# Routed attention and a SiLU layer on one core: the steps of a written-out plan in a new order

## The chip, the cores and the metric

The kernel runs on one core of a Trainium2 chip. The metric is the device time of one execution in microseconds. The core has five engines, each with its own queue of instructions worked off in order: TensorE (PE, matmuls; PEld are its weight loads), VectorE (DVE), ScalarE (ACT), GpSimd (POOL) and SyncE (SP), which here issues the transfers of the DMA engines.

## The reference

Attention in which a query sees only the keys of its own cluster, and after it two matmuls with a SiLU between them:

```
q, k, v: [4, 8, 768, 64]    centroids: [8, 16, 64]
q_assign = argmax over c of (q / |q|) . (centroid / |centroid|)      # k_assign likewise
scores = 1/sqrt(64) * q k^T,  -1e9 where q_assign != k_assign
attn = softmax(scores);  out = attn v                                # [4, 8, 768, 64]
x = out as [3072, 512]
h = x @ w_in        # w_in [512, 2048]
g = h * sigmoid(h)
result = g @ w_out  # w_out [2048, 512], result [3072, 512] in float32
```

## The kernel before

**Tiles.** A batch b (0 to 3) has 8 heads, worked in pairs p (0 to 3). The 768 rows of a head are 6 tiles of 128. Keys and queries of one head pair stand side by side in a buffer `ab` as 24 blocks of 128 columns and 96 partitions in use: 64 carry the scaled number, 32 the code of the cluster (with the rounding rests handled on the way). One score matmul then does both the product and the mask: equal codes leave the score as it is, others push it far down.

**Steps.** `build` makes a graph of 1886 steps. A step is a few instructions on one engine, or one transfer. Each has a tag; these matter here:

- `ld b.p` and `lv b.p`: loads of k or q, and of v, on SyncE (lines 239 and 256). `win n`, `wout n`: loads of the weights (281, 286).
- `p b.p.h.t`: the making of codes for a pair and head. `hi` and `lo` split the float32 numbers into two float16 parts (lines 454 to 461, and 596 and 601 for the first pass of batch 0); `t` turns them, by TensorE for the first pass of batch 0 and by a transposing transfer (line 519) later; `l` are the logits against the centroids (line 534 and others); `L`, `m`, `b`, `o`, `f` are VectorE's sums, maximum, subtraction, one-hot mark and 32 x 32 turn (403, 421, 424, 431, 438); `c` are four copies that put the codes into `ab` (line 190 on VectorE or GpSimd, 188 on ScalarE, 392 as a transfer).
- `a b.h.j`: attention. `S` are scores (687), `E` the exponential (690, ScalarE alone), `V` the products with v (715), `R` and `N` the normalising (734, 739, 745), `X` the turning of the result (762 as a transfer, 772 on TensorE for batch 0), `Y` its copy out of PSUM. `cv` casts v to float16 before that.
- `m b.j`: the two matmuls. `U` (803), tanh `T` (813, ScalarE), gate `G` (816, VectorE), `D` (833), eviction `L` into `ot` (188 or 190) and store `O` (847, SyncE).

Some steps may run on one of several engines: code copies on GpSimd, VectorE, ScalarE or SyncE, casts on GpSimd, VectorE or ScalarE, evictions on ScalarE or VectorE.

**Order.** Nothing of the order is decided when the kernel is built. `PLAN` is a packed list of numbers. Its first 1311 numbers say for every buffer which slot of its pool it takes (8 PSUM banks `M`, 21 `P`, 5 `ab`, 4 `nat`, 8 `gq` and so on); the rest are pairs of a step and the engine chosen. The steps are emitted in that order, so each engine's queue is the list cut down to that engine. A negative number stands for fill matmuls on zeros (line 956), which write to a bank that nobody reads:

```
for at in range(0, len(order), 2):
    n, choice = order[at], order[at + 1]
    if n < 0:
        ...                              # `choice` fill matmuls, line 956
    else:
        s = g.steps[n]
        s.fn(s.engines[choice])
```

Waits follow from the data and from the slots: a step that writes a slot waits until the readers of what stood there have ended. A step that waits holds up all that its engine has behind it in the list; on SyncE a store that waits for its eviction holds up the loads behind it. The list interleaves the batches: TensorE has the matmuls of `m` of one batch between the scores of the next.

Of the kernel before, what the change touches and what calls it, by code (L numbers as in the profile page):

```python
# [16 lines left out]
AX = mybir.AxisListType  # L17


PLAN = (  # L20
    "c-mE(2i%X<`^WF^{aw%C8J@>pS&<S7*~*r^w^U?i&#a2<oxLKP5^0x=6bWTS$R?7NWXtdUIrsT~`TcvneXetzbD#UZ&$+Ja+|T#-cOAduI6nS$QP"
    "1{a`<$Q?pcQsP{Oj_s-}=-aHkO}%ebH+)I`V%(<MI9r*?C;k<2Sg*?=v3H?~C5oXMLW>Z)beyk?q>MIOd9QwC%S~<~>W8b{y?g+A-kbiKQ)n$h=e"
    "7+|x17=$hHQ9-p1t?<ATh4Lj+~*bvwIoMbbT?&~;dxH1KQyjh<B<3na_vT3Q$&lrb(pP4U){y6MZGlygDrtyjP-NI&F{AQgsJ}tgfG}*jmkZWD$3"
    "Nx>+51W3iN0NEspjq7nvl5P33)en>ym>?KnbTnh?at_5txcTib<HT<J;_Ez8u}BXJD|C}d&iom(U@5N^`15yjULx{ynS`dTRZk$UAv3HXuSB%^+6"
    "LA|G&$AyRU9EGJJNQBGD4IeywzfH42$^)%&Ei@tKBRtyi3#)v*x}Fl&*-n0WivL9-J<vs>QS6f=*H_xGM7-n>bWy98MWzkOrZ%%PE<S8t*#wJu2}"
    "5`uOGBX8z6W4%~azoOII?YL;}DQ45yI7l*a=rX%wW5$bP*W4*+uJQIaU}7oB#%D5P6O85Ud)Vxl;!9Z(W8Ta$_s~11jqXS|x>J!|bZnkPc2uhvh>"
    "nQtOr#P>W6W&sBelRWZ~Sl;Z>1j1@kosLjK-Sx37R$Wn>F$xFx9NT&pfjmjTx<1g2{tGG@4?~o`p@Odt+m5&L^Aa*1m+z4#%7L37Slc#H`<}dpeW"
    "DLGxd{&9Sg~ny_8vNL}%sUE`9?GX%_fC)qU&n0qHciiwMmxl^iHC2z(=8v_Abwc^d49aAy9Xjdi%OhiZObBL$+M>9-M7l+SVALV&uzkGI8BiZBaO"
# [86 lines left out]
B, H, S, D = 4, 8, 768, 64  # L115
# [877 lines left out]
```

## Time and profile before

| | |
|---|---|
| median of 3 runs | 299.91 us (299.39 to 299.95) |
| profiled execution | 300.34 us, of which the span of the instructions is 298.6 us |
| TensorE busy | 291.2 us (98%), 3113 matmuls |
| ScalarE, VectorE, GpSimd busy | 230.2, 206.5, 87.6 us |
| queue of SyncE's transfers | 46.82 MB, 63.2% of the 16 engines' span |

The page gives busy time by engine, the span in 40 slices of about 7.5 us (a digit is a busy share in tenths), the chain of work that ended last followed back through what released each step, and groups of instructions with the time of one. TensorE's matmuls are pipelined, so a busy slice says that it had work, not that it was at its peak. A row of waits or of the timeline names the engine, the line, and in brackets how long the engine was idle before and what ended that.

### The profile page before, as it was taken

To read this page: it belongs to the slowest core of one execution; us is meant where nothing else is said; L and a number is where in the kernel's file an instruction comes from. 1 tells how busy PE (TensorE), PEld (TensorE's weight loads), DVE (VectorE), ACT (ScalarE), POOL (GpSimd) and SP (SyncE) were. 2 spreads that over 40 slices of the span, in tenths; PEclk is the share of its full clock that TensorE was granted. 3 is DMA by queue.
4 is the path that set the end of the run, shared out by engine and by line. 5 is a ranking of instruction groups with operands and counts; after the bars stand their busy time and mean duration, and the time that the engine had idled before them with its cause. 6 is when DMAs were issued, how large, how long until landed. Compare 5 with 4: busy or idle time off the path is not lost.

```text
span 298.6 us, 7962 instructions
## 1 busy us (share of the span) xinstructions
PE 291.2 (98%) x3113; PEld 193.6 (65%) x3113; DVE 206.5 (69%) x490; ACT 230.2 (77%) x471; POOL 87.6 (29%) x149
## 2 busy tenths in 40 slices
PE   8889999999999999899999999999999999999995
PEld 6768997876667668556666666566665655555443
DVE  5999988788999899578999746856831230677111
ACT  4999999769899999898898875899999811565112
POOL 4676662344666675431313000012000000000000
PEclk9999999999999999999999999999999999999999
DMA  6999969999999999895549556232202013101013
GB/s 201 308 271 200 348 219 272 292 293 248 266 215 229 266 205 221 248 332 114 111 87 194 131 95 153 67 91 57 61 5 65 0 29 96 74 1 70 2 70 141
DMA packets 81478, 47.36 MB, mean 159 GB/s; under 512 B 58720, under 2 KB 76448, under 8 KB 81440
## 3 DMA queue, kind: packets, MB, share of 16 engines
q1 hardware_dynamic: 81296, 46.82, 63.2%
q8 instruction: 24, 0.39, 0.5%
q14 instruction: 14, 0.11, 0.1%
q10 hardware_dynamic: 144, 0.03, 0.1%
HBM read 27.30 MB, written 6.29 MB: 112 GB/s over the span
## 4 chain that ended last, share of the span: by engine, by line
PE 83%; DMA 7%; ACT 4%; DVE 3%; issue 2%; SPq 1%; POOL 0%; POOLq 0%; ACTq 0%
PE M L833 27%; PE M L803 27%; PE M L687 16%; PE M L715 9%; DMA nv<-in_v_dram 4%; ACT P L690 3%; PE M L534 2%; DMA nat<-in_k_dram 1%; DMA gq<-in_moe_w_out_dram 1%; PE M L956 1%; DVE hl L461 1%; DVE M L424 0%; PE M L772 0%; DVE mx L421 0%; DVE oh L431 0%
## 5 line engine op out<-in xcount | busy, mean ns | idle before, releaser
L690 ACT ACTIVATE P<-M 128x512 f16<-128x512 f32 x288 | 154.3, 662 | 13.1 <-PE M L687 11.5
L803 PE MATMUL M<-xt,win_s 128*128 128x384 f16 (+1 forms) x576 | 96.1, 308 | 0.0
L816 DVE SCALAR_TENSOR_TENSOR gq<-tn,M 128x384 f16<-128x384 f32 (+1 forms) x120 | 66.1, 575 | 39.5 <-ACT tn L813 38.1
L833 PE MATMUL M<-wout_s,gq 128*128 128x512 f16 (+1 forms) x400 | 92.9, 370 | 0.0
L687 PE MATMUL M<-ab 96*128 96x256 f16 (+1 forms) x432 | 90.4, 308 | 0.6 <-ACT P L690 0.3
L813 ACT ACTIVATE tn<-M 128x384 f32<-128x384 f32 (+1 forms) x120 | 60.7, 535 | 22.5 <-PE M L803 18.8
L803 PEld LDWEIGHTS <-win_s 128*128 128x128 f16 x576 | 54.9, 97 | 28.7 <-issue 0.2
L190 POOL COPY ab<-ohT 32x384 f16<-32x384 f16 (+2 forms) x73 | 41.9, 578 | 77.4 <-DVE ohT L438 42.4
L833 PEld LDWEIGHTS <-gq 128*128 128x128 f16 x400 | 37.1, 97 | 36.2 <-DMA gq<-in_moe_w_out_dram 0.2
L715 PEld LDWEIGHTS <-P 128*128 128x128 f16 x1152 | 45.9, 97 | 11.3 <-issue 1.1
L715 PE MATMUL M<-vt,P 128*128 128x65 f16 x1152 | 49.4, 193 | 1.1 <-POOL vt L190 1.1
L687 PEld LDWEIGHTS <-ab 96*128 96x128 f16 x432 | 38.0, 97 | 16.6 <-issue 1.4
L461 DVE SCALAR_TENSOR_TENSOR hl<-nat,hl 128x768 f16<-128x768 f32 (+1 forms) x28 | 27.5, 985 | 0.6 <-POOL hl L458 0.5
L188 ACT COPY ot<-M 128x512 f32<-128x512 f32 (+1 forms) x14 | 8.1, 579 | 22.1 <-PE M L833 22.1
L458 POOL TENSOR_SCALAR hl<-nat 128x768 f16<-128x768 f32 (+1 forms) x19 | 16.4, 862 | 23.9 <-DMA ab<-hl 10.0
L438 DVE STREAM_TRANSPOSE ohT<-oh 128x384 f16<-128x384 f16 (+2 forms) x33 | 18.5, 560 | 1.5 <-POOL ab L190 0.9
L734 DVE RECIPROCAL rz<-M 128x6 f32<-128x6 f32 (+1 forms) x36 | 6.5, 183 | 18.3 <-PE M L715 18.0
L190 DVE COPY ot<-M 128x512 f32<-128x512 f32 (+1 forms) x11 | 7.2, 652 | 15.4 <-PE M L833 15.4
L403 DVE TENSOR_REDUCE M<-M 128x192 f32<-128x384 f32 x24 | 13.4, 559 | 5.8 <-PE M L534 3.6
L190 POOL CAST vt<-nv 128x384 f16<-128x384 f32 x20 | 11.7, 600 | 12.8 <-DMA nv<-in_v_dram 12.2
L745 DVE TENSOR_TENSOR xn<-M,rz 128x384 f16<-128x384 f32 x24 | 13.2, 554 | 0.6
L431 DVE TENSOR_SCALAR oh<-M 128x96 f16<-128x96 f32 (+4 forms) x62 | 13.1, 251 | 0.4
(64 smaller groups left out, 173.7 us busy)
## 6 DMA issues: line engine op xcount, KB each, us to landing
nv<-in_v_dram SPq DMA_DIRECT2D x16, 384.0 KB, 4.5
out_dram<-ot SPq DMA_DIRECT2D x23, 256.0 KB, 2.3
nat<-in_k_dram SPq DMA_DIRECT2D x15, 384.0 KB, 5.4
nat<-in_q_dram SPq DMA_DIRECT2D x12, 384.0 KB, 5.1
gq<-in_moe_w_in_dram SPq DMA_DIRECT2D x8, 512.0 KB, 7.3
gq<-in_moe_w_out_dram SPq DMA_DIRECT2D x8, 512.0 KB, 5.3
nat<-in_q_dram SPq DMA_DIRECT2D x4, 256.0 KB, 6.6
nat<-in_q_dram SPq DMA_DIRECT2D x4, 128.0 KB, 5.6
```

The costliest lines, as they stand in the source:

```text
L190: eng(en).tensor_copy(out, in_)
L403: e.nc.vector.tensor_reduce(out=bank(dst)[:, at : at + HC * n].rearrange("p (n c) -> p n c", c=HC), in_=bank(src)[:, 0 : 32 * n].rearrange ...
L438: e.nc.vector.transpose(T(ohT)[:, 0:n, :].rearrange("p n c -> p (n c)"), T(oh)[:, 0:n, :].rearrange("p n c -> p (n c)"))
L458: e.nc.gpsimd.tensor_scalar(out=dh(), in0=src(), scalar1=QS, scalar2=1.0, op0=ALU.mult, op1=ALU.mult)
L461: e.nc.vector.scalar_tensor_tensor(out=dl(), in0=src(), scalar=QS, in1=dh(), op0=ALU.mult, op1=ALU.subtract)
L687: e.nc.tensor.matmul(bank(sb)[:, at : at + 128 * (c - a)], ab[0:96, kt[m], :], q, start=True, stop=True)
L690: e.nc.scalar.activation(out=T(P)[:, 0:n], in_=bank(sb)[:, 0:n], func=AF.Exp, bias=0.0, scale=ESC)
L715: e.nc.tensor.matmul(bank(O)[:, at : at + D + 1], T(P)[:, c : c + 128], T(vb)[:, VW * m : VW * m + D + 1], start=(m == 0), stop=(m == NJ - ...
L803: e.nc.tensor.matmul(bank(bk)[:, c0 : c0 + n], e.win_s[:, r, ts(fb, 128)], T(X)[:, r, 128 * j0 : 128 * j1], start=(r == 0), stop=(r == NR ...
L813: e.nc.scalar.activation(out=T(tn)[:, 0 : n * per], in_=bank(bk)[:, 0 : n * per], func=AF.Tanh, bias=0.0, scale=1.0)
L816: e.nc.vector.scalar_tensor_tensor(out=gq(f0 // 4)[:, f0 % 4 : f0 % 4 + per, 0:n], in0=T(tn)[:, 0 : n * per].rearrange("p (f c) -> p f c", ...
L833: e.nc.tensor.matmul(bank(bk)[:, 0 : c1 - c0], gq(quarter)[:, fc % 4, ts(t, 128)], e.wout_s[:, fc, c0:c1], start=(fc == 0), stop=(fc == NF ...
```

## The change

Only `PLAN` is another one. Steps, sizes, pools and all other code are the same:

```diff
 PLAN = (
-    "c-mE(2i%X<`^WF^{aw%C8J@>pS&<S7*~*r^w^U?i&#a2<oxLKP5^0x=6bWTS$R?7NWXtdUIrsT~`TcvneXetzbD#UZ&$+Ja+|T#-cOAduI6nS$QP"
...
+    "c-mE&2i%WU8^`beexAp(Jt!o5Z$il4J2Nwq$Se|(y+@I~XDQhkm6=&ciXx+wQAUX*na}(Eo%{U%p4a>N_Pfrw&wcK5uIoDI`M+Mr=QxhX@fvk)l^"
...
 )
```

Unpacked, the two lists hold the same 1886 steps. The new one comes from a search in whose account transposing transfers, code copies made by transfer, and stores hold the DMA queue as long as they did in a trace. What differs when they are set side by side:

- Fill matmuls: 47 in 8 places before (15, 2, 2, 8, 8, 7, 2, 3), 46 in 10 places after (11, 4, 2, 6, 8, 2, 8, 2, 1, 2).
- Engines, as steps of each kind: code copies GpSimd 73, VectorE 27, ScalarE 18, SyncE 14 before, and 78, 29, 12, 13 after; casts of v and the weights GpSimd 32, VectorE 8, ScalarE 8 before, and 28, 13, 7 after; splits `hi` GpSimd 19, VectorE 8, ScalarE 1 before, and 21, 3, 4 after; evictions ScalarE 14, VectorE 11 before, and 12, 13 after. TensorE's steps are the same 685.
- Slots: 1001 of the 1311 buffers take another slot of the same pool.
- Order: every queue differs from its first steps on. The coarse course is the same: the first scores, the first `m` and the pairs of each batch come at about the same place of TensorE's queue.

The stretch of SyncE's queue that the prediction speaks of, in the order of the list:

```
before   ... m0.2O  ld2.3  p2.0.0.0c  p2.1.1.0t  m0.0O  ld2.3  p2.2.1.0t  a1.1.0X  p2.2.0.0t  lv1.3
         p2.3.0.0t  p2.1.0.0c  p2.3.1.0t  lv2.0  a1.5.0X  a1.3.0X  a1.7.0X  ld3.1  ld3.0  p2.2.1.0c ...
after    ... ld2.3 (57th) ... ld2.3 (67th)  p2.1.1.0t  lv1.2  p2.2.1.0t  m0.2O  a1.1.0X  lv1.3  p2.2.0.0t
         m0.0O  p2.3.0.0t  p2.3.1.0t  lv2.0  a1.3.0X  a1.5.0X  a1.7.0X  p2.2.1.0c  ld3.2  ld3.0 ...
```

And its first steps (the sizes in brackets: heads, tiles of 128 rows):

```
before   ld0.0 (2,2) (1,6) (1,6) (2,4)  ld0.1 (2,6) (2,2) (2,4)  ld0.3 (2,6) (2,2)  ld0.2 (2,2) (2,6)  p0.0.0.8t ...
after    ld0.0 (2,2) (1,6) (1,6)  ld0.1 (2,2)  ld0.0 (2,4)  ld0.1 (2,6)  ld0.2 (2,2)  ld0.3 (2,2) (2,6)
         ld0.2 (2,6)  ld0.1 (2,4)  p0.0.0.8t ...
```

More of the change, by code (lines that the diff above doesn't have):

```diff
@@ new lines @@
+    "iGF__2ac2-|Dg!!@c?DFgvZ?mxd(Js&Xtb^jMKEkQG;`-XtAgS0tjY>%mT-|Mj@$37h%)f*Y}@mQKu$jrcF-|9Clemkb#9ZgAnqU=0luoHPMXlD~"
+    "+Mhm~sZ^lZb#&633GgionrH|$i$A6=+edZ~@6VH>;kU$?VMA18rQDV)SIn)GATax|0c%F)8oMbc40PlBa>^I*Na?+dc^O?80yWle;d&~;?O-mwHl"
+    "o{X4xOysN#?!y_Jdr}bbaougHx?_!JgIrA&1>eYQDdl&!cMk(=reQhn>EnelOnqnva9bkD;jTi&*AB4vs&IX-V@$OC(V93W(U2Iz4AnM*0J^8$ga"
+    "E3_#-~!G3)3xE8t1vqv7#<#vfCtiK7&4`g{4#0N)<6`xuCLwRXg{_0_SacfhQqRwl;oxx21W#@_>cue&Dc?f1Ly_S?AzOxb7RBAWi`%-C9e$E<sb"
+    "=@l|-lwh87cg1Hs(Zi@gGkTm|L-(I%6Et)1ntez%-{WI00lR-*^K^po%%GWDjG2MQ%)n#%hJ8sRr_d|P#&n`t;eeTkzBSH#g=5#qXXfifb}=01?z"
@@ new lines @@
+    "%^tXPrpgy1pAo6U&bADz`qI7lM)X@}%(uuiaTsq^}!!iPR_Coa084$3$0>U87j@9<61v`I?|vk90OxqU<^(*qwFEdt%HEx!;vwd?IA_-(#~xlKD#"
+    "cgH|V<i6`xz*ThYniFc3Lw{YHwvT+k*V^!;&Xx7hXRyNtjo!;X&UL0kfbNw%1GK1a}GCS(AZ*#xJ^;|d41kGMK#!o_a^+I-6(;2^4UQ<4Cb6B$ZL"
+    "Z6NDpxv8rE^*9A0lODI^9636_SrphGq)#ABuCq<7f4eV_82GP1>v(ITo;VI(PQ=@-o{Y0nPt%Imm3Y<NI&_GR@7rMna7S6XXh3&yAVDD6qm|BZq5"
+    "ss8KpP*%#G7nyOsf)ErVv~676ZH?4amLj^qb7YbM#8pq)%GGYHsd_nW!78O&#VB4EBT(c}oNyPJEH%-)9V8RRj3;xXUpu2OotHttB_7>Ty~?wFl)"
+    "<1@uP9bg_o<Ew7o^V@F<*^@VD&&pt$m<neckBw%xJsi(oyDn)nw%=x2_at>a#~V4}!)qRX!in^E%xXQZck|NYeBib5?~UZ|keyYyk2`Y6&cj`8U*"
@@ new lines @@
+    "tR8=nwx3S+Dm0-zngJX~24rKayQSb~a8V5`AgD!m)AW*tHACT+r4BBdg~`qRFvd?lotFd%A>U@$q+g>^#D6clEKCyL%V3Gjt+va`Sf3=F!Lg;EkL"
+    "#KKp&)JCnN$PUH;r+4qHa!LgncvTqOB*@tY7@!0Xb)<3*y{K>K3<Tvke(&TA><g{=iJD6ze6YMNgQ`0$h(7Glf+{k>C>UUb$H)))fklUUY_26Nud"
+    "pn7-w~`Dd!+D%c_H@r^&+Jy{{nVh-0BsFjp&QJBxzG^Wz)R2w+Cq1pOHGY(#$q>y&QPD3PD0y36L{5}laA9Kdce!@3N+^nyYPH7>^Ds2ahw-;wki"
+    "5N<be**6TXIdFb+CFN1pA4zKHfmCqr-O15d#Fa0tGGWAG+CU>)Y8dEp2ghp*r@SOEQ)%lGJ8un>;I>+k_Af-JBY`oenNd!O$<i=CP0vZ9wD9~^}7"
+    "FbJN4Z{aZHhu>fz`~*M43OEhtU^(LqM$f=9_!TCaJ@Gn2(53JWY=9-E-s5z}QL?}Qo;^=p4!8hAVVKsMw&B_f^hwAH+cjsEbvB}jkOWiY8|W|S2)"
@@ new lines @@
+    "L;Ipu7Zr!2VEvf&Gd05`7UmLMM0$ey2VgOog|ZPaEpm!Vb#cz<V$Xc0wlVpMcTI@Mvl3Ho{2w2rk1I`8RFT&>L_QR>HeHa|gWw*R{s<DTtnc>F_a"
+    "Jg$eYVh2Da{;3WJ9w_z1z<hi2gHJDA`8Sn@88u=Y<|DZFeQ~d056P)v>;tf_)SV}n?{7ZQgY=-PQbEsQ~{-{T=W8e$yEsAaIl8RIGY4{ZTlwuuwE"
+    "xKDV4qYf0QXlNUp*WONOjFknd=P|JpaATlEhpTC!jyAsO`t1$&Rp}NdEhhbz3Pjd3yQ!!%DI#iu)m}|JL-q~iW&Jd_BM1s9H2c1<=(KB@^e~4C<7"
+    "HB7UCdY^H=VX-(&C7?FoGYifO;0A{1AdJ|)m{P+8xjnDcm@@``85WuXB{@fpTwjy_MhFl|-P#;`&@3Eklt_z<4e`1IL@*5R2-XhXCi+63xiHxk%Q"
+    "p(@ma^3a0%9%wb~71WoXQ`ZtoFlHUS7rQ!IO1V+0=c((7)`Hr4j&d)w75V~fRIH$N(M`}A`*pOEd|E!D{ZM{E`zs!y9ev)^_fX$V>i})28;&-Ish"
@@ L76 @@
+    "v8LIIa5`{4KwQf8Y$9g&QyhCc^jdgYIFBaRogAx0TP~s(e{-sThEh%Gt`7Z~-pDCB+t8Q{L6Sg;-Y@DIbT+y2nz^2$|p~eLFfzXE99Wy^oY<VYKe"
+    "Wx^vO~Gg=yb0%|}_I7eNo&U5TSP#B6pX2=5Np#oHdDv%!vKwc;aW9<Jym=&IaZ14<}ft*kk@_`3p;1A_R#jtW76s4{h+|^#8_t0EuHAsZ}l+&SJC"
+    "=N#`mqlZt96SqtNP?#DfcA&FTVa=g+)xq%&<vgfAG|03K`X%v5C=i13=JS9<Z<HB+K>T4&=5*NbEpH2panFBD2Rr-kN~Zr4YY-pjMWNl0`=f|s1N"
+    "O+J^T+w-Oi{"
 )
```

84 lines of the change are left out of this document (30 added, 54 removed).

## The prediction

> **What bounds the kernel now.** I read the page first: the share of busy time, the slices, and the chain that ended last.
>
> ```profile
> PE 291.2 (98%) x3113; PEld 193.6 (65%) x3113; DVE 206.5 (69%) x490; ACT 230.2 (77%) x471; POOL 87.6 (29%) x149
> PE   8889999999999999899999999999999999999995
> DMA  6999969999999999895549556232202013101013
> PE 83%; DMA 7%; ACT 4%; DVE 3%; issue 2%; SPq 1%; POOL 0%; POOLq 0%; ACTq 0%
> ```
>
> TensorE is busy for 291.2 of 298.6 us, and 83% of the chain is its own work. An order changes no amount of work, so what it can win lies in the 7.4 us without it: the slices show them at the start, in the sixteenth slice (about 120 us), and at the end. Then I asked for the stretches of time and for what TensorE waited for.
>
> ```profile
> core 0: us, PE busy (x) PEld busy (x) DVE busy (x) ACT busy (x) POOL busy (x), PEclk, DMA share, GB/s
> 13.00:26.00 13.00, 11.91 (x184) 9.69 (x182) 12.43 (x32) 12.63 (x28) 9.78 (x18) 1.00 1.15 259
> 50.00:85.00 35.00, 35.00 (x362) 24.76 (x360) 30.29 (x67) 29.79 (x57) 16.24 (x20) 1.00 1.01 270
> 85.00:102.00 17.00, 17.00 (x223) 11.62 (x221) 15.64 (x35) 16.43 (x34) 12.26 (x17) 1.00 1.03 253
> 102.00:111.70 9.70, 9.69 (x146) 6.69 (x145) 9.02 (x22) 9.60 (x21) 6.79 (x9) 1.00 1.18 204
> 119.00:124.00 5.00, 3.93 (x67) 3.02 (x66) 3.99 (x15) 4.11 (x9) 2.50 (x5) 1.00 0.84 172
> PE M L581 <- DMA nat<-in_q_dram: 0.9, 2, 0.6
> PE M L715 <- POOL vt L190: 1.1, 1, 1.1
> ```
>
> From 13 to 26 us ScalarE (12.63 of 13) and VectorE (12.43) are full and TensorE is not: there the exponentials set the pace. From 50 to 111.7 us TensorE is full and VectorE has 4.71 + 1.36 + 0.68 = 6.75 us idle. In 119 to 124 us TensorE loses 5.00 - 3.93 = 1.07 us, the one wait of 1.1 us for a cast of v. That is the only stall after the first 30 us worth a term. The chain and the timeline tell how it came about.
>
> ```profile
> 102.74 0.58 SPq L847 DMA_DIRECT2D out_dram<-ot  x1
> 103.36 0.42 SPq L239 DMA_DIRECT2D nat<-in_k_dram  x1
> 109.92 2.02 SPq L519 DMA_TRANSPOSE ab<-hl  x1
> 110.72 0.98 DVE hl L461
> 112.04 0.81 SPq L392 DMA_DIRECT2D ab<-ohT  x1
> 112.96 2.44 SPq L519 DMA_TRANSPOSE ab<-hl  x1
> 115.49 5.64 DMA nv<-in_v_dram
> 116.13 4.96 SPq L762 DMA_TRANSPOSE xt<-xn  x3
> 121.25 0.50 POOL L190 CAST vt<-nv 128x384 f16<-128x384 f32 x1 [2.47 <-DMA nv<-in_v_dram]
> 121.81 0.52 PE L715 MATMUL M<-vt,P 128*128 128x65 f16 x12 [1.07 <-POOL vt L190]
> ```
>
> SyncE issues one thing after the other: the second half of ld2.3 behind a store, then, through the split that VectorE ends at 110.72 + 0.98 = 111.70, the transposing transfers p2.3.0.0t (109.92) and p2.3.1.0t (112.96) with a code copy between them (112.04), then lv2.0 (115.49). It lands at 121.13, the cast follows, and the products a2.0.0V wait for it.
>
> **The change part by part.** The new list has the same 1886 steps; fill matmuls go from 47 to 46. I set both lists side by side by step.
>
> Start, up to the first 21 exponentials (they fill the 21 P buffers). ScalarE has ahead of them 8 splits, 2 moves, 3 code copies and 1 cast in both lists, and one centroid placement less (3 for 4), which VectorE takes. VectorE also takes one split and one more turn of x while TensorE does its first 21 us of work.
>
> ```profile
> L188 ACT COPY st<-M 64x32 f16<-64x32 f16 (+1 forms) x8 | 1.6, 203 | 0.1
> L456 DVE TENSOR_SCALAR hl<-nat 128x768 f16<-128x768 f32 x8 | 5.3, 659 | 0.3 <-issue 0.3
> L190 DVE COPY xt<-M 128x256 f16<-128x256 f16 x9 | 2.5, 284 | 0.7 <-PE M L772 0.7
> 1.04 3.38 PE L956 MATMUL M<-zeros 128*128 128x256 f16 x15 [1.04 <-DVE zeros L195]
> 4.21 0.97 PE L581 MATMUL M<-ident,nat 128*128 128x128 f32 x4
> 12.91 0.60 ACT L690 ACTIVATE P<-M 128x512 f16<-128x512 f32 x1
> 9.46 0.71 PE L956 MATMUL M<-zeros 128*128 128x256 f16 x5
> ```
>
> A placement is two copies: 2 x 0.203 = 0.41 us off ScalarE, which is the bound there. VectorE gains 0.41 + 0.66 + 0.28 = 1.35 us against 13.00 - 12.43 = 0.57 us of idle, so up to 0.78 us may come out as delay, because TensorE's score banks wait for VectorE too. On SyncE the loads for pairs 3 and 2 move ahead of the late part of q for pair 1; these are the loads for which TensorE waited 0.9 us. So the start lies between -1.3 (0.41 and 0.9 both won) and +0.8; the two signs rest on nearly full engines, and I take 0. The first fill goes from 15 to 11 matmuls; it stands before the first transposes (4.21), which wait for a load, so it costs nothing by itself.
>
> The stall at 121 us. Both halves of ld2.3 move up on SyncE (from 70th and 74th place to 57th and 67th), so the store at 102.74 no longer stands before them. The code copy at 112.04 leaves SyncE for GpSimd, so p2.3.1.0t follows p2.3.0.0t directly: 112.96 - 112.04 = 0.92 us earlier, if its split is ready. The first a2.0.0V keeps its place in TensorE's queue (the matmuls ahead of it are worth the same within 0.1 us). But ahead of that split (p2.3.1.0lo) VectorE now has more to do: one more maximum chain, two more evictions of ot, four more code copies, one more cast of v, the placement; less one split and two turns of x.
>
> ```profile
> L421 DVE TENSOR_REDUCE mx<-M 128x12 f32<-128x192 f32 (+2 forms) x33 | 11.4, 345 | 0.7
> L424 DVE TENSOR_TENSOR M<-M,mx 128x192 f32<-128x192 f32 (+2 forms) x33 | 11.6, 354 | 0.8
> L403 DVE TENSOR_REDUCE M<-M 128x192 f32<-128x384 f32 x24 | 13.4, 559 | 5.8 <-PE M L534 3.6 <-ACT xt L188 0.9 <-ACT P L690 0.9
> L431 DVE TENSOR_SCALAR oh<-M 128x96 f16<-128x96 f32 (+4 forms) x62 | 13.1, 251 | 0.4
> L190 DVE COPY ot<-M 128x512 f32<-128x512 f32 (+1 forms) x11 | 7.2, 652 | 15.4 <-PE M L833 15.4
> L190 DVE COPY ab<-ohT 32x384 f16<-32x384 f16 (+2 forms) x27 | 8.2, 308 | 0.7
> L190 DVE CAST vt<-nv 128x384 f16<-128x384 f32 x6 | 2.6, 426 | 0.0
> ```
>
> That is (0.345 + 0.354 + 0.559 + 2 x 0.251) + 2 x 0.652 + 4 x 0.308 + 0.426 + 0.406 - 0.659 - 2 x 0.284 = 3.9 us more. Call r what of it fits into idle time. The stall is then 1.07 + 0.1 - 0.92 + (3.9 - r) = 0.25 + 3.9 - r, not below 0. The idle time there was 6.75 us, and the loads behind some of it come earlier, so I take r = 3.9: the stall shrinks from 1.07 to 0.25, a gain of 0.8. Its ends are a gain of 1.07 and, with r = 0, a loss of 3.1.
>
> 124 us to the last matmul. TensorE is full in every slice; steps exchanged there are hidden by its queue. DMA's slices are mostly at 4 to 6 tenths to about 187 us and at 3 or fewer after, so a load or transpose that moves has room. I cost it at 0; without that cover each late transfer would cost its own delay, and the 0.25 left above already stands for one.
>
> The tail. The last piece, 128 columns, is evicted by ScalarE behind two 512-column copies; before it was VectorE's, free since long.
>
> ```profile
> 294.12 0.58 ACT L188 COPY ot<-M 128x512 f32<-128x512 f32 x1 [0.23 <-PE M L833]
> 295.44 0.29 DVE L190 COPY ot<-M 128x128 f32<-128x128 f32 x1 [3.87 <-PE M L833]
> ```
>
> The second 512-column copy takes 0.58, and the last three groups of four 128-column matmuls run beside it and cover most of that; the copy of 128 columns was 0.29 on VectorE and is between that and 0.58 on ScalarE, so 0 to +0.3. I take +0.1, nearer to the row of the same shape.
>
> Sum: 0 - 0.8 + 0 + 0.1 = -0.7 us. The profiled execution took 300.34 us (span 298.6 and 1.74 around it), which gives 299.6; the median of the runs, 299.91, lies 0.43 below it, so in the median's terms 299.2 us. 0.2% is 0.6 us here, about what a measurement can tell from no change.
>
> **The rivals.** *The stall stays (no change).* lv2.0 needed 5.64 us from issue to landing with three transposing transfers of x right behind it (116.13), and in the new list the same three follow it again, the first even readier. If that is what delays it, the 0.92 us on SyncE are lost again. For it: no other row explains 5.64. Against: it was issued late. Time: 299.91 + 0.1 = 300.0.
>
> *VectorE falls behind (slower).* Nothing else has work added on a nearly full engine that works in strict order. If its idle time was waiting for results and not for work, r is small: at r = 0 the stall is 4.15 us and the time 299.9 + 3.1 + 0.1 = 303.1; it turns slower by over 0.2% where r is below about 2.7, and a middle case, r = 1.7, gives 301.4. For it: in 102 to 111.7 us only 0.68 us are idle. Against: 4.71 us of the idle time lie earlier, from 50 to 85 us.
>
> *The clock of TensorE rises later.* In the first fill 15 matmuls took 3.38 us, 0.23 each; at 9.46 five took 0.71, 0.14 each with the tail of the last. The granted clock is shown as 1.00 throughout, so only the pace tells of it. With 11 matmuls the fill ends at about 3.5 us and TensorE pauses until the load has landed at 4.2; if the rise counts from there, it comes some 3 us later, and the transposes (0.97 at the slow pace), the logits and the placement until 8 us run at half pace: up to +1.2, that is 300.4. For it: the pause is new. Against: VectorE's work lies between those steps and hides part. The Trainium skill says on its page "TensorE: Matmul & The Clock Gate", section "Part 1: The HAM clock gate", that the clock is released after a busy window of about 3.4 us and that the window runs free of the kernel's start; by that rule the pause could cost a window or nothing, run by run, and the trace agrees in that the transposes at 4.21, over 3 us after the first matmul, still ran at the slow pace; the window's phase no run here shows. By the rule at its worst the sum would be 300.4 instead of 299.2.
>
> **How the numbers follow.** My forecast, the stall largely gone and the start unchanged or a little better: 0.45, with its own range 297.6 to 299.3. The stall stays or start and stall cancel: 0.29, and the late clock 0.06, together 0.35 for no measurable change. VectorE behind, here or at the start: 0.20. The low end is the full 1.07 with the start's 1.3, less the tail: 299.91 - 1.07 - 1.3 + 0.1 = 297.6; the high end is r = 1.7, 301.4; the rest of the slower case stays outside, under 0.1, and as much below.
>
> **What would show it.** Right: the wait of TensorE for vt near 120 us is under 0.4 us, p2.3.1.0t follows p2.3.0.0t on SyncE without a pause, VectorE's idle time from 50 to 112 us falls to about 3 us, and the first exponential still starts near 12.9 us. Wrong: VectorE over 98% busy from 85 to 112 us with TensorE below full; lv2.0 landing over 5 us after its issue; the first exponential later than 13.5 us, or matmuls at the 0.21 us pace beyond 5 us; a new wait of over 0.5 us after 124 us.

## The result and the profile after

The new list takes 303.02 us (median of 4 runs, 302.64 to 304.12) against 299.93 us (4 runs, 299.39 to 301.09): a ratio of 1.0104, 95% interval 1.0064 to 1.0143. It is slower by 3.1 us. The profiled execution took 302.93 us. From the page of the new list, the span and TensorE's and VectorE's slices (tenths of busy time in 40 slices of 7.5 us):

```profile
span 301.1 us, 7968 instructions
PE 292.9 (97%) x3112; PEld 193.7 (64%) x3112; DVE 207.8 (69%) x494; ACT 229.2 (76%) x465; POOL 87.5 (29%) x153
...
PE   8999999999999989899999999999999999999995
...
DVE  4999988888999999768978784476573130756220
```

Before, the only 8 of TensorE after the start stood at 119 us, with the wait for lv2.0; now there is another at 105 us. The windows of the prediction, for the new list (window, its length, then busy time and instructions of each engine):

```profile
50.00:85.00 35.00, 34.93 (x353) 25.11 (x351) 31.54 (x65) 29.90 (x59) 16.09 (x22) 1.00 1.05 250
85.00:102.00 17.00, 16.97 (x228) 11.21 (x225) 16.52 (x39) 15.76 (x32) 9.82 (x16) 1.00 1.19 271
102.00:111.70 9.70, 8.86 (x123) 5.57 (x120) 9.47 (x21) 8.71 (x19) 6.20 (x11) 1.00 1.07 248
119.00:124.00 5.00, 4.01 (x92) 3.27 (x89) 4.93 (x17) 4.95 (x10) 0.98 (x3) 1.00 1.17 166
```

From 102 to 111.7 us VectorE is busy for 9.47 of 9.70 us (98%) while TensorE, 9.69 before, falls to 8.86. The prediction had named VectorE over 98% busy from 85 to 112 us with TensorE below full as a sign of being wrong; from 85 to 111.7 us it is 25.99 of 26.70 us (97%), just short of that. Other signs of that kind came in full: lv2.0 landed 6.18 us after its issue, and the first exponential started at 14.27 us. TensorE's waits in the new list (engine, line, released by; us, times, longest):

```profile
PE M L715 <- POOL vt L190: 1.0, 1, 1.0
PE M L715 <- DVE oh L431: 0.6, 1, 0.6
PE M L687 <- DVE oh L431: 0.4, 1, 0.4
...
PE M L687 <- DVE M L403: 0.2, 1, 0.2
PE M L687 <- DVE ab L190: 0.2, 1, 0.2
```

The wait for vt is still there, and four waits for VectorE are new (so are one of 0.3 for a transposing transfer and one of 0.2 for ScalarE, not shown). Both lists were profiled a second time. The table says how late TensorE is: the end of a matmul in the trace, less the undisturbed length of all matmuls ahead of it in the list (each shape at its usual spacing).

| us of the trace | before, two profiles | new, two profiles | difference of the means |
|---|---|---|---|
| up to 28 | 8.01, 8.17 | 8.16, 8.52 | +0.25 |
| 28 to 50 | 0.81, 0.94 | 1.52, 1.69 | +0.73 |
| 50 to 105 | 0.74, 1.17 | 0.95, 1.52 | +0.28 |
| 105 to 112 | 0.27, 0.11 | 1.26, 1.47 | +1.18 |
| 112 to 126 | 1.53, 1.17 | 1.62, 1.48 | +0.20 |
| 126 to 290 | 1.52, 1.53 | 1.88, 1.92 | +0.37 |
| start of the last matmul to the end | 3.38, 3.37 | 3.56, 3.58 | +0.19 |

The sum is +3.2 us, less 0.1 for the fill matmul that is gone: the 3.1 measured. Two losses are large, at 28 to 50 and at 105 to 112 us; and the wait at 121 us, which was to go, stayed. The places in the new list's timeline (start, length, engine, line; in brackets the idle time before):

```profile
28.37 1.85 DVE L190 COPY ab<-ohT 32x512 f16<-32x512 f16 x4
30.34 0.26 DVE L421 TENSOR_REDUCE mx<-M 128x8 f32<-128x128 f32 x1
31.37 0.82 PE L687 MATMUL M<-ab 96*128 96x256 f16 x6 [0.44 <-DVE oh L431]
105.87 0.83 POOL L458 TENSOR_SCALAR hl<-nat 128x768 f16<-128x768 f32 x1
105.93 1.36 DVE L190 COPY ab<-ohT 32x384 f16<-32x384 f16 x2
107.70 0.56 DVE L190 CAST vt<-nv 128x384 f16<-128x384 f32 x1
109.04 0.53 PE L715 MATMUL M<-vt,P 128*128 128x65 f16 x12 [0.61 <-DVE oh L431]
112.22 4.57 SPq L519 DMA_TRANSPOSE ab<-hl  x2
114.49 0.95 DVE L461 SCALAR_TENSOR_TENSOR hl<-nat,hl 128x768 f16<-128x768 f32 x1
116.83 1.01 SPq L256 DMA_DIRECT2D nv<-in_v_dram  x1
123.14 0.50 POOL L190 CAST vt<-nv 128x384 f16<-128x384 f32 x1 [3.96 <-DMA nv<-in_v_dram]
123.69 0.52 PE L715 MATMUL M<-vt,P 128*128 128x65 f16 x12 [0.99 <-POOL vt L190]
```

At 28 us VectorE does four code copies in a row, and the maximum chain whose bank TensorE needs (p0.2.0.8) stands behind them. At 106 us two code copies take 1.36 us beside GpSimd's split, then a cast 0.56, and one-hot marks for TensorE stand behind. At 114.49 comes the split p2.3.1.0lo, which ended at 111.70 before; p2.3.1.0t waits for it at 115.50 with SyncE idle from 113.64, and lv2.0 is queued behind that.

How much VectorE had done when that split ended, in both lists (a window from the start to the split's end, then three of its groups in that window; before first):

```profile
0.00:111.70 111.70, 108.55 (x1404) 83.20 (x1405) 97.62 (x239) 100.62 (x202) 64.96 (x110) 1.00 1.02 255
L461 DVE SCALAR_TENSOR_TENSOR hl<-nat,hl 128x768 f16<-128x768 f32 (+1 forms) x20 | 19.7, 989 | 0.5 <-POOL hl L458 0.5
L190 DVE COPY ab<-ohT 32x512 f16<-32x512 f16 (+2 forms) x13 | 4.2, 325 | 0.3
L190 DVE CAST vt<-nv 128x384 f16<-128x384 f32 x2 | 0.9, 433 | 0.0
...
0.00:115.44 115.44, 111.62 (x1423) 84.45 (x1424) 103.11 (x250) 101.99 (x203) 65.48 (x115) 1.00 1.04 252
L461 DVE SCALAR_TENSOR_TENSOR hl<-nat,hl 128x768 f16<-128x768 f32 (+1 forms) x20 | 21.3, 1065 | 0.1
L190 DVE COPY ab<-ohT 32x256 f16<-32x256 f16 (+2 forms) x17 | 6.6, 388 | 0.5
L190 DVE CAST vt<-nv 128x384 f16<-128x384 f32 x3 | 1.9, 635 | 0.0
```

VectorE's busy time ahead of the split's end rose by 103.11 - 97.62 = 5.49 us and its idle time fell from 14.08 to 12.33 us, so the split ended 3.74 us later. In the second profiles (b_same and a_same below) the busy time rose by 6.89 us, the idle time fell by 2.60, and the split ended 4.29 us later.

### The profile page after: what moved, and what is told of

It is laid out like the page before. It is cut to its first block, busy times and chain, and to the rows that moved or that the text cites. A ratio compares the mean times of both kernels' runs of the same rounds, so it can differ in the third digit from the quotient of the medians.

```text
span 301.1 us, 7968 instructions
## 1 busy us (share of the span) xinstructions
PE 292.9 (97%) x3112; PEld 193.7 (64%) x3112; DVE 207.8 (69%) x494; ACT 229.2 (76%) x465; POOL 87.5 (29%) x153
## 4 chain that ended last, share of the span: by engine, by line
PE 83%; DVE 9%; DMA 4%; issue 1%; ACT 1%; POOL 0%; SPq 0%; DVEq 0%; POOLq 0%
PE M L833 27%; PE M L803 26%; PE M L687 17%; PE M L715 9%; DMA nv<-in_v_dram 2%; PE M L534 2%; DVE hl L461 2%; DMA ab<-hl 2%; DVE lo L601 1%; PE M L956 1%; DVE ab L190 1%; DVE gq L816 1%; DVE oh L431 1%; PE M L581 1%; DVE mx L421 1%
## 5 line engine op out<-in xcount | busy, mean ns | idle before, releaser
L690 ACT ACTIVATE P<-M 128x512 f16<-128x512 f32 x288 | 154.6, 636 | 15.7 <-PE M L687 13.5
L833 PE MATMUL M<-wout_s,gq 128*128 128x512 f16 (+2 forms) x400 | 93.7, 370 | 0.0
L461 DVE SCALAR_TENSOR_TENSOR hl<-nat,hl 128x768 f16<-128x768 f32 (+1 forms) x28 | 29.6, 1057 | 0.1
L458 POOL TENSOR_SCALAR hl<-nat 128x768 f16<-128x768 f32 (+1 forms) x21 | 17.7, 841 | 34.4 <-DMA nat<-in_q_dram 30.6
L188 ACT COPY ot<-M 128x512 f32<-128x512 f32 (+1 forms) x12 | 6.8, 565 | 11.9 <-PE M L833 11.8
L190 DVE COPY ot<-M 128x512 f32<-128x512 f32 (+1 forms) x13 | 8.7, 667 | 9.4 <-PE M L833 9.4
L431 DVE TENSOR_SCALAR oh<-M 128x96 f16<-128x96 f32 (+4 forms) x62 | 13.2, 252 | 0.6
L745 DVE TENSOR_TENSOR xn<-M,rz 128x384 f16<-128x384 f32 x24 | 13.2, 548 | 0.3
L534 PEld LDWEIGHTS <-ab 128*128 128x128 f16 x288 | 10.2, 96 | 2.9 <-DMA ab<-hl 0.6
```

The source lines that it names most:

```text
L190: eng(en).tensor_copy(out, in_)
L458: e.nc.gpsimd.tensor_scalar(out=dh(), in0=src(), scalar1=QS, scalar2=1.0, op0=ALU.mult, op1=ALU.mult)
L461: e.nc.vector.scalar_tensor_tensor(out=dl(), in0=src(), scalar=QS, in1=dh(), op0=ALU.mult, op1=ALU.subtract)
L534: e.nc.tensor.matmul(bank(Lb)[:, 32 * i : 32 * i + 32], a, st, start=True, stop=True)
L690: e.nc.scalar.activation(out=T(P)[:, 0:n], in_=bank(sb)[:, 0:n], func=AF.Exp, bias=0.0, scale=ESC)
L833: e.nc.tensor.matmul(bank(bk)[:, 0 : c1 - c0], gq(quarter)[:, fc % 4, ts(t, 128)], e.wout_s[:, fc, c0:c1], start=(fc == 0), stop=(fc == NF ...
```

## The experiments

Each run was timed against the kernel before on the same chip; "+1.6" is the difference of the medians there. The new list stands at +2.5 to +3.1. The 12 executions of one kernel spread over 1.4 to 3.5 us, once 5.1, so a profile, which is one execution, may lie 1 us off the median. In a_lv2, a_dve, a_fill and b_lv2 the plan takes three lines less, and line numbers are 3 lower.

**Both lists again.** No edit.

> The new list unchanged, a second profile and more times. If the losses belong to the list and not to one execution: time 302.5 to 303.3, TensorE's waits at 30 to 31.4, 106 to 109 and 122 us are there again, each within 0.4 us, and lv2.0 needs over 5.5 us. If they were of that execution: 301.0 to 302.

303.08 us, ratio 1.0089 (1.0061 to 1.0117). Its waits repeat (0.80 for the one-hot mark, 1.07 for vt), and lv2.0 took 6.26 us. The losses belong to the list.

> The list before unchanged, a second profile. lv2.0 took 5.64 us in the first one, but 3.67 and 4.04 in two near copies of this list with the same issue within 0.4 us. If the long landing belongs to the list: 5 us or more again and a wait near 1 us at 121. If it belongs to the execution: it may land within 4.2 us, the wait is under 0.3 us and the profiled execution is about 1 us shorter than the first.

300.70 us, ratio 1.0008 (0.9979 to 1.0036). lv2.0 took 5.06 us, the wait was 0.50: long again, but this list's wait varies between executions.

**VectorE at 106 us, taken off and put on.**

```diff
 a_dve: the new list
-VectorE: p1.3.1.0c, p2.0.0.0c (105.93), cv1.2 (107.70)
+GpSimd:  p1.3.1.0c, p2.0.0.0c, cv1.2
 b_dve: the list before
-GpSimd:  p1.3.1.0c twice (105.10), cv1.2 (108.33)
+VectorE: p1.3.1.0c twice, cv1.2
```

> The new list with three engine choices changed, nothing moved: the two code copies and the cast that VectorE does from 105.93 to 107.28 and from 107.70 to 108.27 us (0.88 + 0.44 + 0.56 = 1.88 us) go to GpSimd. Theory 'VectorE falls behind': TensorE's waits of 0.23 and 0.61 us at 106 and 109 us, both for VectorE, shrink to under 0.2 together, the split p2.3.1.0lo (114.49) comes 1 us or more earlier and lv2.0 with it; TensorE is 0.8 to 1.9 us earlier at 130 us, time 301.1 to 302.2. Rival 'ScalarE or the score banks are the bound there' or 'GpSimd becomes late with 1.5 us more': time 302.7 to 303.5, and the waits go over to GpSimd or ScalarE.

302.04 us, +1.6, ratio 1.0047 (1.0013 to 1.0080): about 1 us of the 3 is back. TensorE is full there again, and loses 0.12 us from 105 to 112 instead of 1.26:

```profile
102.00:111.70 9.70, 9.70 (x135) 6.34 (x132) 8.45 (x21) 9.50 (x20) 9.20 (x14) 1.00 1.10 256
```

VectorE is down to 8.45 us and GpSimd up to 9.20. The wait for lv2.0 is unchanged (0.97): TensorE reaches it earlier, and lv2.0 lands 1.0 us earlier. How much of the loss at 106 to 109 us belongs to these three steps is not exact: TensorE's wait for the one-hot mark there, 0.61 and 0.80 us in the two profiles of the new list, was 0.46, 0.45, 0.30 and 0.17 in a_lv2, a_split, a_fill and a_put30 below, which leave these steps as they are. It also depends on what went before.

> The list before with three engine choices changed to what the new list has there: two code copies p1.3.1.0c (GpSimd 105.10 to 106.14 us) and one cast of cv1.2 (108.33 to 108.83) go to VectorE. Undisturbed these take 2 x 0.25 + 0.35 = 0.85 us of VectorE's time, beside GpSimd's copies up to 1.9. Theory 'VectorE has no room from 102 to 112 us': TensorE waits for VectorE there and is 0.5 to 1.5 us later at 112 us, or the split p2.3.1.0lo and with it lv2.0 come later and the wait at 121 us grows by as much; time 300.4 to 301.4. Rival 'the room before is enough, r = 3.9': time 299.9 within 0.3.

300.36 us, +0.2, ratio 1.0001 (0.9979 to 1.0023). By its time the rival holds, by its trace the theory. The window in b_dve:

```profile
102.00:111.70 9.70, 8.93 (x135) 5.89 (x134) 9.44 (x23) 9.49 (x19) 4.30 (x6) 1.00 1.04 238
```

and TensorE's wait in its timeline:

```profile
111.33 0.38 PE L687 MATMUL M<-ab 96*128 96x512 f16 x1 [0.53 <-DVE xn L745]
```

Three small pieces of work cost TensorE 1.21 us from 105 to 112 us where the list before loses 0.11 to 0.27. There was no room on VectorE. But TensorE then starts the products that need lv2.0 at 121.08 us without a wait; before it was free for them at 120.74 and had to wait until 121.81. Where TensorE waits anyway, coming later by less than the wait costs nothing, so the wait at 121 us could cover the loss. The trace does not show that alone: in this execution lv2.0 also landed early (119.52, after 4.04 us), which by itself takes the wait away, and at 28 us TensorE was 0.6 us less late than in before. How much of the loss the wait covered stays open.

**The price of a copy beside GpSimd.** A kernel with these instructions alone, no attention and no matmuls of the reference.

> Only copies, casts and splits of the kernel's shapes, in stretches that VectorE has alone, GpSimd has alone, and both share; everything else is left out. Theory 'VectorE and GpSimd keep each other out when both copy in SBUF': VectorE's code copy (32 x 384) takes 0.25 us alone and 0.5 us or more from start to start beside GpSimd's, the cast 0.35 and 0.6 or more, the split with two SBUF inputs 0.92 and 1.2 or more, while the copy out of PSUM (128 x 512) takes 0.69 in both. Rival 'the long copies of the trace are only the profile's start marks': the same time from start to start in both.

Its timeline (start, length, then the group). Of VectorE's rows the first, fourth, sixth and eighth are alone, the third runs beside GpSimd's splits, the others beside GpSimd's code copies; of GpSimd's rows the first is alone, the second beside VectorE's code copies:

```profile
8.06 2.25 DVE L960 COPY ab<-ohT 32x384 f16<-32x384 f16 x8
17.50 6.64 DVE L960 COPY ab<-ohT 32x384 f16<-32x384 f16 x12
25.75 8.58 DVE L960 COPY ab<-ohT 32x384 f16<-32x384 f16 x12
35.48 2.33 DVE L963 CAST vt<-nv 128x384 f16<-128x384 f32 x6
39.05 4.58 DVE L963 CAST vt<-nv 128x384 f16<-128x384 f32 x8
46.25 3.94 DVE L966 SCALAR_TENSOR_TENSOR hl<-nat,hl 128x768 f16<-128x768 f32 x4
51.42 5.84 DVE L966 SCALAR_TENSOR_TENSOR hl<-nat,hl 128x768 f16<-128x768 f32 x5
61.59 2.87 DVE L972 COPY ot<-M 128x512 f32<-128x512 f32 x4
65.69 4.32 DVE L972 COPY ot<-M 128x512 f32<-128x512 f32 x6
...
11.27 5.08 POOL L960 COPY ab<-ohT 32x384 f16<-32x384 f16 x9
17.26 7.33 POOL L960 COPY ab<-ohT 32x384 f16<-32x384 f16 x13
```

A code copy takes 2.25 / 8 = 0.28 us alone, 6.64 / 12 = 0.55 beside GpSimd's code copies, and beside its splits (25.75; eight of them) 0.88 by single records. A cast takes 0.39 alone and 0.57 beside copies, the split 0.98 and 1.17, the copy out of PSUM 0.72 both times. GpSimd's copies take 5.08 / 9 = 0.56 from start to start alone and 7.33 / 13 = 0.56 beside VectorE's copies; beside VectorE's splits their single records last 1.11 instead of 0.50. The Trainium skill, on its page "SBUF — State Buffer", section "Who interferes with whom", says that VectorE's copies and casts in its two-port modes, and its instructions with two inputs in SBUF, contend with GpSimd for a shared pair of ports, and that an instruction with at most one input in SBUF, outside those modes, does not. These rows agree: of VectorE's instructions here, the copy out of PSUM, which has no input in SBUF, is the one that stays the same. It also says that one blocks the other for the whole instruction; 12 copies of 0.28 and 13 of GpSimd's at 0.56 would then take 10.7 us one after the other, and both were done in 7.33, so the measured overlap decides.

**When lv2.0 is issued.**

```diff
 a_split: the new list
-VectorE: a1.4.0N, p2.1.1.0L, m, b, o, p2.3.1.0lo
+VectorE: a1.4.0N, p2.3.1.0lo, p2.1.1.0L, m, b, o
 a_lv2: the new list
-SyncE: p2.3.0.0t, p2.3.1.0t, lv2.0
+SyncE: p2.3.0.0t, lv2.0, p2.3.1.0t
 b_lv2: the list before
-SyncE: p2.3.0.0t, p2.1.0.0c, p2.3.1.0t, lv2.0
+SyncE: p2.3.0.0t, lv2.0, p2.1.0.0c, p2.3.1.0t
 b_899: the list before
-SyncE: p2.1.0.0c (112.04)
+GpSimd: p2.1.0.0c
```

> The new list with one step moved on VectorE: the split p2.3.1.0lo goes from behind the evictions, the maximum chain of p2.1.1.0 to directly behind a1.4.0N, the place that it has in the list before; the amount of VectorE's work ahead of TensorE's waits stays the same. Theory 'order, not amount, makes lv2.0 late': the split ends near 113.3 instead of 115.44, p2.3.1.0t is issued by 113.7 and lv2.0 by 115.2, and of the 0.99 us wait at 122.7 at least 0.7 is gone; the 0.61 us wait at 108 stays; time 302.0 to 302.4. Rival 'the transfers decide the landing': lv2.0 is issued 1.5 us earlier and still lands after 122; time 302.7 to 303.3. Third: the chain of p2.1.1.0 is now 0.95 us later and TensorE waits for it instead; time 303 within 0.3.

302.44 us, +1.9, ratio 1.0055 (1.0029 to 1.0080). The split ended at 113.36, 2.1 us earlier, and p2.3.1.0t followed p2.3.0.0t at once. But it then held SyncE for 2.44 us instead of 1.28, so lv2.0 went out at 116.63, only 0.2 us earlier. The wait for vt is gone all the same, because the landing took 3.83 us (120.45). The order of the split is thus not what makes lv2.0 late by itself. The third expectation came as well: TensorE waits 0.64 us at 113.89 for p2.1.1.0L, which now stands behind the split.

```profile
113.89 0.38 PE L687 MATMUL M<-ab 96*128 96x256 f16 x2 [0.64 <-DVE M L403]
```

> The new list with one step moved on SyncE: the load lv2.0 goes ahead of the transposing transfer p2.3.1.0t instead of behind it. In the new list SyncE stood idle from 113.64 to 115.50 us because that transfer waited for VectorE's split, and lv2.0 (issued 116.83, landed 123.01) was queued behind it. Theory 'issued late': lv2.0 goes out near 113.7, lands by about 120, TensorE's wait of 0.99 us before 123.69 is gone, time 303.0 - 1.0 = 302.0. Rival 'the transfer is slow wherever it is issued, because the transposing transfers around it hold the queue': it lands at 122 or later, at least 0.5 us of the wait is left, time 302.5 to 303.0.

302.05 us, +1.6, ratio 1.0045 (1.0015 to 1.0075). lv2.0 went out at 114.56 and landed at 118.47; the wait is gone and nothing took its place (0.27 us lost from 112 to 126).

> The list before with one step moved on SyncE: lv2.0 goes ahead of the code copy p2.1.0.0c and the transposing transfer p2.3.1.0t, to about 112.0 us instead of 115.49. Theory 'issued late': it lands by about 118, TensorE's wait of 1.07 us at 121 is gone, time 299.9 - 1.0 = 298.9, and no other wait takes its place. Rival 'slow wherever it is issued': it lands near 121 again, time 299.7 to 300.0.

300.09 us, -0.4, ratio 0.9981 (0.9949 to 1.0012). The wait at 121 us is gone (landing at 117.08), but p2.3.1.0t went out 0.75 us later, and 0.86 us is lost between 115 and 122, of it 0.28 by its logits. The time does not tell it from before.

> The list before with one engine choice changed: the code copy p2.1.0.0c that SyncE issues as a transfer at 112.04 us goes to GpSimd, the step on which the forecast's 0.92 us rested. Theory 'SyncE's order sets lv2.0': p2.3.1.0t is issued near 112.0, lv2.0 near 114.6 and the wait at 121 us falls from 1.07 to 0.2 to 0.4, time 299.1 to 299.3. Rival 'the transfers in the queue set it': lv2.0 is issued 0.9 us earlier and lands less than 0.4 us earlier, time 299.7 to 300.0.

299.51 us, -0.7, ratio 0.9970 (0.9950 to 0.9990): the forecast's step alone gives the forecast's time. Its way is another one:

```profile
109.84 5.19 SPq L519 DMA_TRANSPOSE ab<-hl  x2
115.13 0.53 SPq L256 DMA_DIRECT2D nv<-in_v_dram  x1
```

The two transposes follow each other without a pause, but the second then takes 2.71 us to issue, and lv2.0 goes out only 0.36 us earlier than before, not 0.92. It landed at 118.80, 2.33 us earlier: the landing took 3.67 us instead of 5.64.

**What makes a landing long.** The trace records each packet. lv2.0 is 256 packets of 1536 bytes. In microseconds:

| run | issue | last packet ends | landing | issue to landing | 16 KB packet of instructions starts |
|---|---|---|---|---|---|
| before | 115.49 | 119.17 | 121.13 | 5.64 | 119.17 |
| b_same | 116.27 | 119.78 | 121.33 | 5.06 | 119.24 |
| new list | 116.83 | 121.10 | 123.01 | 6.18 | 121.10 |
| a_same | 118.16 | 122.51 | 124.42 | 6.26 | 122.51 |
| a_dve | 115.87 | 120.08 | 121.98 | 6.11 | 120.08 |
| b_dve | 115.48 | 119.04 | 119.52 | 4.04 | 118.85 |
| b_899 | 115.13 | 118.44 | 118.80 | 3.67 | 118.81 |
| a_split | 116.63 | 120.06 | 120.45 | 3.83 | 120.61 |
| a_lv2 | 114.56 | 117.85 | 118.47 | 3.91 | 119.72 |

In before, the packets that start between 119.2 and 121.1 us are all smaller than lv2.0's, so its data had been moved for 2 us when the cast was let go:

```profile
DMA packets 258, 0.07 MB, mean 35 GB/s; under 512 B 258, under 2 KB 258, under 8 KB 258
```

In the 0.1 us ahead of that stretch one packet of the instruction queue began (queue: packets, MB, share of 16 engines):

```profile
q8 instruction: 1, 0.02, 59.9%
```

The long landings have that packet at or just before the end of lv2.0's last packet; a_fill (6.25) and a_put30 (5.66) too. The trace also has the 16 marks by which a load is reported as done. In these seven landings 14 or 15 of the 16 came together 0.8 to 0.9 us after the packet of instructions had ended (before: the packet ended at 120.13, 14 marks came from 120.91 to 121.13). In b_dve the packet began at the same place, but 15 marks came from 119.30 to 119.52 while it was still being moved (until 120.24), and the landing was short. Two kernels were to move the packet:

```diff
-one matmul of 256 columns, `choice` times
+`choice` // 2 matmuls of 512 columns, and one of 256 if it is odd
```

> The list before with its fills in half as many matmuls of twice the columns (25 instead of 47; the same time in the fills, the memory of zeros is twice as wide and about 0.1 us longer to clear). TensorE's program is 22 matmuls, 44 instructions, shorter ahead of 121 us, so its 16 KB of code are fetched some 0.9 us later against the work. Theory 'the code packet holds up lv2.0's landing': the fetch starts after 119.8 us, lv2.0 lands 4.2 us or less after its issue, TensorE's wait at 121 us is under 0.3 us, time 299.1 to 299.4 where before has 300.2 to 300.5 beside it. Rival 'the turns of x issued right behind lv2.0 hold it up': it needs over 5 us again and the wait is 0.5 us or more, time within 0.3 of before.

299.44 us, -1.0, ratio 0.9958 (0.9937 to 0.9979), the lowest median of this study. lv2.0 took 3.95 us (issue 114.84, last packet 118.28, landing 118.79), the instruction packet started at 118.71, TensorE lost 0.42 us from 112 to 126 instead of 1.17 to 1.53.

> The new list with its fills in half as many matmuls of twice the columns (24 instead of 46), as in b_code. Theory 'code packet': the fetch that began at 121.10 us begins near 122, lv2.0 lands 4.3 us or less after its issue instead of 6.2, the wait of 0.99 us is gone, time 301.9 to 302.3. Rival 'turns of x': 6 us again, time 302.8 to 303.2.

302.52 us, +2.1, ratio 1.0053 (1.0026 to 1.0080). lv2.0 took 4.29 us, the packet started at 123.59 after the landing at 123.34, and no wait for vt was left.

Both landings were short, as the theory of the instruction packet had said, with x's turns issued right behind lv2.0 as always, which speaks against that rival. But the edit did not move the packet as expected. In b_code it was to start after 119.8 us and started at 118.71; counted from lv2.0's issue it came 0.2 us later than in before, and lv2.0's last packet 0.2 us earlier. In a_code lv2.0 was issued 2.2 us later than in the new list, in an execution that was late from the start (TensorE waited 1.44 us for a transposing transfer at 27 us, a wait of 0.3 and 0.5 in the two profiles of the new list); from the issue the packet came 0.3 us later and lv2.0's last packet 0.4 us earlier. So a shift of a few tenths of a us between the two went with the short landings, and that the edit made this shift is not shown. With b_dve as an exception, the theory is not settled. What holds the landing back until after the packet, no run here shows.

**The start.**

```diff
 a_fill: first fill of the new list
-11 matmuls
+15 matmuls
 a_put30: the new list
-VectorE: p0.3.1.0c (28.84), p0.1.0.8c (29.89)
+GpSimd:  p0.3.1.0c, p0.1.0.8c
```

> The new list with 15 matmuls instead of 11 in the first fill, as the list before has it; nothing else. In the new list the matmuls kept the slow pace (0.21 us) until about 6.5 us, before until about 5.0. Theory 'the clock rises late because of the shorter first fill': fast pace again by about 5.0 us, first exponential near 13.2 instead of 14.27, time 302.1 to 302.8. Rival 'the start is lost elsewhere, in VectorE's order of work at 28 to 31 us': the first exponential may come earlier, but TensorE still waits for VectorE at 30 to 31.4 us (0.19 + 0.44) and the time stays at 303.0 within 0.3. Third, 'the rise does not depend on the first fill': slow pace until 6 us or later.

303.17 us, +2.7, ratio 1.0080 (1.0050 to 1.0110). The profile shows TensorE 0.5 to 0.8 us less late at 28 us (7.70), but the first exponential still started at 14.03 us, not near 13.2, the waits at 30 us are there again, and the time is that of the new list: no gain that the runs can tell.

> The new list with two engine choices changed near 29 us: of the four code copies that VectorE does in a row from 28.37 to 30.23 us (0.46 to 0.55 each, beside copies and casts of GpSimd), the second and the fourth go to GpSimd. Theory 'the start is lost because VectorE's chain p2.., here p0.2.0.8 (maximum, threshold, one-hot), stands behind copies': TensorE's waits of 0.19 and 0.44 us at 30.00 and 31.37 us shrink to under 0.2 together, TensorE is 0.4 to 0.9 us earlier at 40 us, time 302.1 to 302.6. Rival 'GpSimd is as full there': the copies come later on GpSimd, the scores for pair 3 wait for them instead, time 302.9 to 303.5.

302.62 us, +2.4, ratio 1.0062 (1.0032 to 1.0093). In the trace both waits are gone and TensorE loses 1.07 us from 28 to 50 instead of 1.52 and 1.69; the time is 0.1 to 0.7 us under the new list's, less than these intervals can tell from nothing.

**All together, and the best of before.**

```diff
 a_all: the new list with a_fill, a_put30, a_dve and a_lv2
 b_best: the list before
-SyncE: p2.3.0.0t, p2.1.0.0c, p2.3.1.0t, lv2.0
+SyncE: p2.3.0.0t, lv2.0, p2.3.1.0t
+GpSimd: p2.1.0.0c
```

> The new list with all four repairs at once: first fill of 15, the two code copies near 29 us and the two code copies and the cast near 106 us on GpSimd, lv2.0 ahead of p2.3.1.0t. If the repairs hit separate losses they add: 0.46 (fill, by TensorE's lateness at 35 us), 0.5 (29 us), 1.1 (106 us) and 1.2 (lv2.0) off 303.0 give 299.8, that is level with the list before or a little under it. If they overlap (what one wins is taken by the next wait), 300.5 to 301.5.

301.88 us, +1.7, ratio 1.0037 (1.0009 to 1.0065): they do not add; the time is that of a_lv2 or a_dve alone. All the waits aimed at are gone, and a new one came at once, in the up-projection behind VectorE's gate:

```profile
133.65 3.41 PE L803 MATMUL M<-xt,win_s 128*128 128x384 f16 x20 [0.49 <-DVE gq L816]
```

TensorE lost 1.1 us from 130 to 140. The profiled execution was the fastest of its 12 (300.70), so where the typical one loses the other 1.2 us stays open.

> The list before with p2.1.0.0c on GpSimd (as b_899) and lv2.0 ahead of p2.3.1.0t as well. lv2.0 goes out near 112.3 and lands by 117, so no length of its landing can make TensorE wait; p2.3.1.0t is 0.6 us later than in b_899 and still 0.5 earlier than in b_lv2, where its logits waited 0.28 us. Expected: no wait over 0.2 us from 115 to 126 us, time as b_899 (0.7 under before) or up to 0.2 less. If the later transposing transfer costs: a wait of 0.2 to 0.4 us at 119 us, 0.4 under before.

299.65 us, -0.8, ratio 0.9971 (0.9950 to 0.9993). lv2.0 landed at 116.33; 0.52 us was lost between 112 and 120 (0.2 of it logits that waited for their transpose), 0.11 after. As fast as b_899, not faster. b_899, b_best and b_code beat both lists.

## Why the prediction was wrong

**The step that failed is the term 3.9 - r with r = 3.9**, "so I take r = 3.9": the added work was to fit whole into VectorE's idle time. Both of its numbers were wrong. The work ahead of the split p2.3.1.0lo cost VectorE 5.49 us more (6.89 in the second pair of profiles), not 3.9, and only 1.75 us of it (2.60) went into idle time. The difference is the 3.74 us (4.29) by which the split came later. From 50 to 111.7 us alone VectorE's idle time fell from 6.75 to 4.17 us, where the prediction expected about 3, and of what is left 3.46 us lie before 85 us. Work that becomes ready at 100 us cannot be done at 70. The trace had said so: 0.68 us idle from 102 to 111.7. In b_dve three small pieces put there cost TensorE 1.21 us.

**The price was a mean, and old work became dearer.** Code copies stood in the sum at 0.308 and the cast at 0.426 us. The three that were put at 106 us took 0.88, 0.44 and 0.56, beside splits and a cast on GpSimd. Up to the split the group of code copies, with four more, grew by 2.4 us instead of 1.2, and that of casts, with one more, by 1.0 instead of 0.4. The same 20 splits on VectorE, which had no term, took 21.3 us instead of 19.7 (23.2 instead of 19.9 in the second pair); port shows such a split at 0.98 alone and 1.17 beside GpSimd's copies, but which of the 20 grew for that reason was not followed.

**The place of the loss was not in the formula.** The delay was to show at the wait for lv2.0. Most of it came earlier, as waits of 0.23 and 0.61 us behind VectorE at 106 and 109 us. So TensorE reached lv2.0 later, and the wait there, with lv2.0 landing 1.88 us later, was 0.99 us instead of the 0.25 foreseen. The two places together (105 to 126 us) cost +1.38 instead of -0.8.

**The 0.92 us on SyncE did not come.** The code copy left SyncE, but p2.3.1.0t did not follow p2.3.0.0t: it waited 1.86 us for its split. "If its split is ready" was the condition, and the same paragraph had the reason why it was not. And where the split was in time (b_899, a_split), the second of two transposes held SyncE for longer, and lv2.0 gained 0.36 and 0.2 us, not 0.92: the step priced the copy's slot on SyncE and took it that the second transpose would hold SyncE no longer when it follows the first directly; it took 2.71 and 2.44 us there, against 1.28 after a pause in the new list. Done alone it gave -0.7 us, though mostly by a shorter landing.

**Start 0** (ends -1.3 and +0.8) came out at +0.98 up to 50 us, past its end. TensorE's wait for a load before 8.53 us went, as weighed, but ScalarE's first exponential started at 14.27 and 14.36 us, later than the 13.5 named as a sign. The larger part, 0.73, was VectorE's again: copies ahead of the chain that TensorE needs. The prediction had looked at the sum of work up to the first exponentials, not at the order at 28 us.

**124 us to the end, 0**, was +0.37, and **the tail, +0.1**, +0.19: small, both to the slower side. "TensorE is full in every slice; steps exchanged there are hidden by its queue" had no term for the short waits that came: in both profiles of the new list one at 145 us, of 0.2 and 0.1 us, which the list before does not have. Where the rest of the 0.37 lies was not followed.

**The rivals.** "VectorE falls behind" had 0.20 and 301.4 to 303.1 us; VectorE did fall behind, and 303.02 lies at its r = 0 end. That the number fits is luck in part: r was not 0, the work was larger than its 3.9, and its formula puts all 3.1 us into the wait for lv2.0, where 105 to 126 us cost 1.38 and the rest was lost at the start and late. The range stopped at r = 1.7 and missed. "The stall stays" was right that something besides the issue delays lv2.0: 5.06 to 6.26 us in all four profiles of the two lists. "The clock rises later" was seen in the pace: in the new list the transposes at 5.33 us still took 1.06 us for four, and the first matmuls at full pace came at 4.9 to 6.9 us in six profiles with the fill of 11, at 4.2 to 6.2 in eight with 15. But load and first transposes came sooner too, without the pause that was foreseen, and a_fill shows no gain in time. The Trainium skill, page "TensorE: Matmul & The Clock Gate", section "Part 1: The HAM clock gate", has the window run free of the kernel's start; a spread of 2 us for the same start of the list, in the six profiles with the fill of 11, agrees with that.

A slip without effect: the slice at 120 us is the seventeenth, not the sixteenth.

## What to carry to other kernels

Idle time of an in-order engine is worth only what lies between the moment when the added work becomes ready and the moment when its follower is needed: read it in that window, not in a wider one. Price a copy on VectorE by its row beside the GpSimd work that will run next to it, and ask what that GpSimd work does to the instructions that were there before. When the same steps are in both lists, compare an engine's busy time up to the step that matters: it shows at once whether the work or the room was misjudged. A wait that already stands behind a place can cover what is lost ahead of it, so the price of a change in one list need not be its price in another; b_dve fits this but does not prove it.

## What the runs showed of the hardware

- The transposing transfers p2.3.0.0t and p2.3.1.0t kept SyncE for 4.6 to 5.5 us from the first's start to the second's end: 5.19 (b_899) and 4.89 (a_split) with nothing between them, 4.57 with 1.86 of waiting between them (new list), 5.48 with a code copy between them (before).
- VectorE's code copy took 0.28 us alone and 0.55 beside GpSimd's copies, from start to start, and 0.88 as a single record beside GpSimd's splits; GpSimd's copy, as a single record, 0.50 alone and 1.11 beside VectorE's splits (all in port).
- A load whose packets had all been moved was seen as landed 0.4 to 0.9 us later in nine profiles, and 1.5 to 2.0 us later in seven, in all of which a 16 KB packet of instructions was moved at the end of it (one of the nine, b_dve, had such a packet too). Filling TensorE with half as many matmuls of twice the width, of no use in themselves, went with the short landing at 121 us and, in the list before, a gain of 1.0 us.
